# Moving sums from VectorE to GpSimd, two chunks' transposes from TensorE to VectorE and two chunks' keys through DRAM, with a new order of all steps

## The chip, the cores and the metric

The kernel runs on one NeuronCore of a Trainium2 chip. Its engines are TensorE (PE; PEld is its weight load), VectorE (DVE), ScalarE (ACT), GpSimd (POOL) and SyncE (SP), which here issues all the DMAs. The metric is the device time of one execution in microseconds (us), lower is better: before the change 535.64 us, the median of 3 runs (535.61 to 535.70).

## The reference

Two blocks follow each other. The first is a gated linear recurrence over 768 tokens, for 4 batches and 8 heads of 48 dimensions; the second is a feed-forward layer with the hardswish activation over the 3072 tokens that come out:

```python
for t in range(S):                                   # q, k, v, alpha: (4, 8, 768, 48)
    state = alpha[:, :, t, :, None] * state + einsum('bhd,bhe->bhde', k[:, :, t], v[:, :, t])
    y[:, :, t] = einsum('bhd,bhde->bhe', q[:, :, t], state)
x = y.transpose(0, 2, 1, 3).reshape(3072, 384)
h = x @ w_in                                         # (384, 2048)
g = h * clip(h + 3, 0, 6) / 6
out = g @ w_out                                      # (2048, 384)
```

## The kernel before

**Chunks.** The recurrence is done in 24 chunks of 128 tokens, six to a batch. For a chunk j the kernel needs alpha, k and q with the dimensions of a pair of heads on the partitions and tokens along the free axis. For chunks below FIRST (6) they arrive as tokens by dimensions and TensorE turns them (`transposed`, L274, four transposes of 128x128 for each of `ta`, `tk`, `tq`; ScalarE copies the turned alpha out, L300). From chunk FIRST on they arrive in a layout of 32x32 blocks (`load_akq`, four DMAs for each of alpha, k and q) and VectorE turns the blocks (`by_blocks`, L285, words `ca`, `tk`, `tq`). Two scans on VectorE give the running products of alpha (`r`, L309, and `p`, L320), and `scaled` (words `k` and `q`, L332) multiplies keys and queries by them.

**Attention of a chunk.** `sc` (L346) makes the scores on TensorE, `m` (L356) masks them on VectorE, `u` (L429) makes the update of the state, which `sm` (VectorE), `st` (L409, GpSimd) and `sv` (ScalarE) carry on, and `ya`, `yb` (L455) make the output, which `cy` copies to the feed-forward's input. `u` needs the keys by token. Below chunk FAR (8) TensorE turns the scaled keys back (`kb`, L374) and ScalarE copies them (`ck`). From FAR on VectorE turns 32x32 blocks (`kt`, L391), four DMAs write them to DRAM (`kw`, L396) and four read them back in the other layout (`kr`, L404).

**Feed-forward.** Tokens are taken in groups g of two chunks. The weights arrive as 64-bit numbers and are made into float32 by `d1`, `d2`, `dx` (ScalarE), `d3` (VectorE) and `d4` (L217, GpSimd). Group 0 and group 1 use plain products in the first layer (`fa`, `fb`, `f`), group 0 also in the second (`b`, L516). The other layers use schemes with fewer multiplications, in exchange for sums:

- First layer, groups 2 to 11: sums of weight blocks once (`y`, L577) and of input blocks for each group (`xc`, L586, 11 sums of 128x128), 20 products (`M`, L592 to L602, eight matmuls each), eleven products kept by ScalarE (`n`, L606), then 12 sums of 128x512 (`o`, L608; step 0 of outputs 2, 3, 6 and 7 adds two kept products, both in SBUF, and the last step adds a product that is still in PSUM). `e` (L494, ScalarE) and `h` (L498, VectorE) make the activation.
- Second layer, groups 1 to 11: sums of weight blocks once (`x`), sums of activations (`s`, L658: four of 128x512, one of 128x1024, one of two times 128x512), seven products (`P`, L685, sixteen matmuls each), copies `K` and sums `G` out of PSUM, stores `O`.

**Order.** The order is written out by hand as one long string of words (L751 to L900). A word is one call, such as `M.2.7.0` for product 7 of group 2 in PSUM bank 0. Each engine, and SP's DMA queue, takes its instructions in that order, and an instruction that waits holds back everything behind it on its engine. `z` is TensorE work without a use; 26 such products stand in the first 20 us, mostly ahead of and between the first chunks' transposes. PSUM has eight banks of 128x512: four are `banks` (attention), four are `bank_m` (feed-forward).

## Time and profile before

| | |
|---|---|
| median of 3 runs | 535.64 us |
| span of the profiled execution, first to last instruction | 533.7 us |
| the median over that span | 1.9 us |
| PE busy (6306 instructions) | 524.6 us |
| VectorE busy (849) | 477.2 us |
| ScalarE busy (503) | 257.2 us |
| GpSimd busy (71) | 50.4 us |
| granted TensorE clock | 1.00 throughout |
| DMA, 16 engines, mean share | 42.5% |

The span is a single profiled execution. Busy time of PE counts a matmul from its start to its modelled end, and matmuls overlap, so the rate of PE is read from the distance between the ends of equal instructions. VectorE's instructions overlap a little too: one of 0.68 us is followed by the next after 0.60 us.

### The profile page before, as it was taken

The page shows a single profiled execution, that of the slowest core. Times are in us where ns is not written, and L with a number is a line of the kernel's source. Part 1 is how long each engine was busy: PE and PEld are TensorE (multiplying, and loading weights), DVE is VectorE, ACT ScalarE, POOL GpSimd, SP SyncE. Part 2 cuts the span into 40 slices and gives each one's busy share as a digit, 9 for nine tenths or more (in the row PEclk, how much of TensorE's full clock was granted, in tenths as well). Part 3 has the DMA queues.
Part 4 walks back from the last instruction along what each step waited for, and adds up shares of the span by engine and source line. Part 5 has one row for each costly group of instructions (what it writes and reads, how often), then busy time and mean ns, then how long its engine had stood idle before and what let it go on. Part 6 is the DMA issues. An engine that isn't in the chain of part 4 may idle for free.

```text
span 533.7 us, 15143 instructions
## 1 busy us (share of the span) xinstructions
PE 524.6 (98%) x6306; PEld 499.4 (94%) x6306; DVE 477.2 (89%) x849; ACT 257.2 (48%) x503; POOL 50.4 (9%) x71
## 2 busy tenths in 40 slices
PE   8799999999999999999999999999999999999997
PEld 7698886789999999999999999999999999999997
DVE  6999989999999999998999999999999899496382
ACT  3889865212653553553544444642634544553340
POOL 5333425100000000000000000000000000000000
DMA  9998876005615155254344355044454042100001
GB/s 174 217 252 256 215 216 152 21 2 154 152 30 116 32 121 135 57 140 95 87 110 113 91 124 140 19 120 102 115 136 104 11 110 43 44 2 2 15 16 37
DMA packets 124100, 54.40 MB, mean 102 GB/s; under 512 B 83328, under 2 KB 116864, under 8 KB 124032
## 3 DMA queue, kind: packets, MB, share of 16 engines
q1 hardware_dynamic: 124032, 53.44, 42.5%
q8 instruction: 49, 0.80, 0.6%
q14 instruction: 19, 0.16, 0.1%
HBM read 44.50 MB, written 8.91 MB: 100 GB/s over the span
## 4 chain that ended last, share of the span: by engine, by line
PE 85%; DVE 8%; POOL 2%; DMA 2%; ACT 1%; issue 1%; SPq 1%; DVEq 0%; POOLq 0%
PE m_ps L703 34%; PE m_ps L600 34%; PE m_ps L478 5%; PE t_ps L455 4%; PE t_ps L346 2%; PE t_ps L429 2%; PE m_ps L489 2%; PE t_ps L282 1%; DVE rings L647 1%; DMA v<-in_v_dram 1%; DVE raw L537 1%; ACT raw L191 1%; DMA kq<-in_k_dram 1%; DVE g_sb L647 1%; DVE w L537 1%
## 5 line engine op out<-in xcount | busy, mean ns | idle before, releaser
L606 ACT COPY g_sb<-m_ps 128x512 f32<-128x512 f32 x110 | 63.6, 584 | 124.9 <-PE m_ps L600 104.1
L703 PE MATMUL m_ps<-w,g_sb 128*128 128x192 f32 x704 | 121.7, 327 | 0.0
L703 PEld LDWEIGHTS m_ps<-w,g_sb 128*128 128x128 f32 x704 | 113.7, 190 | 0.4
L703 PE MATMUL m_ps<-rings,g_sb 128*128 128x192 f32 x528 | 91.5, 326 | 0.0
L703 PEld LDWEIGHTS m_ps<-rings,g_sb 128*128 128x128 f32 x528 | 85.4, 190 | 0.1
L600 PE MATMUL m_ps<-xc,w 128*128 128x128 f32 x640 | 82.7, 277 | 0.3 <-DVE w L541 0.3
L600 PEld LDWEIGHTS m_ps<-xc,w 128*128 128x128 f32 x640 | 77.5, 192 | 1.5 <-issue 0.5
L494 ACT ACTIVATE r<-g_sb,half 128x512 f32<-128x512 f32 x80 | 56.8, 722 | 32.9 <-DVE g_sb L541 12.1
L498 DVE SCALAR_TENSOR_TENSOR g_sb<-r,g_sb 128x512 f32<-128x512 f32 x80 | 53.6, 682 | 4.6 <-ACT r L494 4.2
L600 PE MATMUL m_ps<-xT,raw 128*128 128x128 f32 x400 | 52.5, 277 | 0.0
L600 PEld LDWEIGHTS m_ps<-xT,raw 128*128 128x128 f32 x400 | 48.6, 192 | 0.6
L409 POOL TENSOR_TENSOR st<-sm,R 128x192 f32<-128x192 f32 x20 | 12.9, 643 | 353.8 <-DVE sm L439 306.7
L647 DVE TENSOR_TENSOR g_sb<-g_sb 128x512 f32<-128x512 f32 (+1 forms) x55 | 42.0, 795 | 0.2
L600 PE MATMUL m_ps<-xT,w 128*128 128x128 f32 x320 | 42.0, 276 | 0.0
L600 PEld LDWEIGHTS m_ps<-xT,w 128*128 128x128 f32 x320 | 39.3, 192 | 0.1
L366 ACT COPY A<-q 48x256 f32<-48x256 f32 x88 | 35.5, 404 | 5.0 <-DVE q L332 3.7
L356 DVE TENSOR_TENSOR A<-t_ps,mask 64x256 f32<-64x256 f32 x96 | 36.0, 414 | 0.4
L478 PE MATMUL m_ps<-xT,w 128*128 128x256 f32 x144 | 32.8, 382 | 0.0
L600 PE MATMUL m_ps<-xc,raw 128*128 128x128 f32 x240 | 31.8, 276 | 0.0
L309 DVE TENSOR_TENSOR_SCAN R<-t,ones 128x516 f32<-128x516 f32 x24 | 29.7, 1236 | 1.1 <-ACT t L300 1.0
L478 PEld LDWEIGHTS m_ps<-xT,w 128*128 128x128 f32 x144 | 26.7, 190 | 3.6
L600 PEld LDWEIGHTS m_ps<-xc,raw 128*128 128x128 f32 x240 | 29.6, 192 | 0.1
(104 smaller groups left out, 731.0 us busy)
## 6 DMA issues: line engine op xcount, KB each, us to landing
raw<-in_moe_w_out_dram SPq DMA_DIRECT2D x8, 768.0 KB, 5.2
raw<-in_moe_w_in_dram SPq DMA_DIRECT2D x6, 768.0 KB, 6.8
v<-in_v_dram SPq DMA_DIRECT2D x48, 96.0 KB, 3.0
out_dram<-oh SPq DMA_DIRECT2D x44, 96.0 KB, 1.7
far<-kq SPq DMA_DIRECT2D x64, 64.0 KB, 2.2
kb<-far SPq DMA_DIRECT2D x64, 64.0 KB, 2.0
aq<-in_alpha_dram SPq DMA_DIRECT2D x36, 96.0 KB, 2.5
qq<-in_q_dram SPq DMA_DIRECT2D x36, 96.0 KB, 2.4
```

The source lines that it names most:

```text
L309: nc.vector.tensor_tensor_scan(out=reverse(R, n - 1, n), data0=reverse(ax, n, n), data1=reverse(ones, n, n), initial=0.0, op0=ALU.mult, op ...
L356: nc.vector.tensor_tensor(out=to[:, a], in0=sc[a][half], in1=mask[half, half].unsqueeze(1).to_broadcast([HB, NP, HB]), op=ALU.mult)
L366: nc.scalar.copy(out=to[:, a], in_=Q_t[j][64 * a : 64 * a + D, :, half])
L409: nc.gpsimd.tensor_tensor(out=st, in0=sm, in1=R_t[j][:, :, 0:1].to_broadcast([C, NP, D]), op=ALU.mult)
L455: nc.tensor.matmul(y_of(j, (i + 1) // 2, p)[:, HB * b : HB * b + HB], vb[:, p, e : e + 32], A_t[j][:, b, 2 * p + a], start=(b == 0 and i = ...
L478: nc.tensor.matmul(h[:, f], w1[:, kk, o : o + C], xT_t[g][:, kk], start=(kk == 0), stop=(kk == KT - 1))
L494: nc.scalar.activation(out=to, in_=h, func=AF.Relu, bias=half, scale=1.0 / 6.0)
L498: nc.vector.scalar_tensor_tensor(out=to, in0=r, scalar=1.0, in1=h, op0=ALU.min, op1=ALU.mult)
L600: nc.tensor.matmul(acc[g][i][:, f * C : (f + 1) * C], spots[w][:, f * C : (f + 1) * C], x_of(g, x), start=(first and f == 0), stop=last, s ...
L606: nc.scalar.copy(out=slots[z], in_=acc[g][i])
L647: nc.vector.tensor_tensor(out=out, in0=in0, in1=in1, op=ALU.subtract)
L703: nc.tensor.matmul(to[g], a, rhs[:, f], start=(first and f == 0), stop=(last and f == HF - 1), skip_group_check=True)
```

## The change

- `FIRST` goes from 6 to 4: alpha, k and q of chunks 4 and 5 arrive in blocks and are turned by VectorE. Their six sets of four TensorE transposes and two ScalarE copies go; six VectorE block transposes come, and 24 DMAs of a quarter each in place of 6.
- `FAR` goes from 8 to 6: the keys of chunks 6 and 7 go through DRAM. Two sets of four TensorE transposes and two ScalarE copies go; two VectorE block transposes and 16 DMAs come.
- Words with a `g` in front (`gx`, `gy`, `gxc`, `go`, `gs`, `gk`, `gq`) run the same function with GpSimd in place of VectorE. The order uses 8 `gy`, 62 of the 110 `xc`, 30 of the 120 `o`, 38 of the 66 `s`, and 11 keys and 14 queries of `scaled`. That is 100 instructions of 128x512, 6 of 128x1024 and 62 of 128x128. All of them read two operands in SBUF.
- The eight PSUM banks are one set, `banks`, for attention and feed-forward.
- The order of the 1788 words is new from the first to the last. Apart from the `g` and the bank numbers the words are the same, but for `ta` of chunks 4 and 5 and `kb` and `ck` of chunks 6 and 7, which go, and `kt`, `kw` and `kr` of chunks 6 and 7, which come.

```diff
-    banks = [ps.tile([C, NP * C], FP, tag=f"t{i}", name=f"t{i}_ps") for i in range(4)]
+    banks = [ps.tile([C, NP * C], FP, tag=f"t{i}", name=f"t{i}_ps") for i in range(8)]
...
-    FIRST = 6
+    FIRST = 4
...
-        nc.vector.tensor_tensor(out=t, in0=src, in1=by, op=ALU.mult)
+        lane[0].tensor_tensor(out=t, in0=src, in1=by, op=ALU.mult)
...
-    FAR = 8
+    FAR = 6
...
-    bank_m = [ps.tile([C, GT * 2], FP, tag=f"m{i}", name=f"m{i}_ps") for i in range(4)]
...
-    def add(eng, out, in0, s0, in1, s1):
-
+    lane = [nc.vector]
+
+    def on_gpsimd(f):
+        def g(*at):
+            lane[0] = nc.gpsimd
+            f(*at)
+            lane[0] = nc.vector
+        return g
+
+    def add(out, in0, s0, in1, s1):
+        eng = lane[0]
...
-                nc.vector.tensor_tensor(out=t, in0=part(a21, i), in1=part(a22, i), op=ALU.add)
+                lane[0].tensor_tensor(out=t, in0=part(a21, i), in1=part(a22, i), op=ALU.add)
...
+    for name in ("x", "y", "xc", "o", "s", "k", "q"):
+        steps["g" + name] = on_gpsimd(steps[name])
...
-        run("""z.0.5 z.0.3 z.0.1 z.0.8 qa.0.0 w.0 d2.0 d3.0 la.0 ta.0.0 ca.0 r.0 lk.0 tk.0.1 k.0
-               z.0.2 p.0 la.1 ta.1.2 lq.0 tq.0.3 ca.1 r.1 lk.1 lv.0.0 sv.0.0 d1.0 kb.0.0 ck.0 z.0.2
...
+        run("""z.7.2 z.7.3 z.2.5 w.0 d2.0 d3.0 z.7.3 z.1.2 z.2.8 la.0 ta.0.7 ca.0 z.7.2 la.1 ta.1.0
+               ca.1 lq.0 tq.0.7 z.2.1 lk.0 tk.0.5 z.2.3 d1.0 dx.0 lk.1 w.2 r.0 p.0 q.0 qa.0.1 d1.2
...
+               sc.6.3.6 la.8 ca.8 K.1.2 gxc.2.1 gxc.2.3 gxc.2.10 gy.16 gy.17 gy.12 kr.6 u.6.5.7
...
+               m.8 gs.2.4 ca.11 M.3.9 o.3.1.0 n.3.5.10 P.2.5 tk.10 lq.11 e.3.1.1 h.3.1 sc.9.3.5
...
```

## The prediction

> **What bounds the kernel now.** I read the page first, its busy times and its 40 slices.
>
> ```profile
> span 533.7 us, 15143 instructions
> PE 524.6 (98%) x6306; PEld 499.4 (94%) x6306; DVE 477.2 (89%) x849; ACT 257.2 (48%) x503; POOL 50.4 (9%) x71
> ...
> PE   8799999999999999999999999999999999999997
> DVE  6999989999999999998999999999999899496382
> ```
>
> PE is busy all the time, and VectorE nearly so up to slice 32 (430 us). Next, who PE waited for (the view of waits, for PE alone):
>
> ```profile
> PE m_ps L532 <- POOL ident masks.py:199: 1.5, 1, 1.5
> PE t_ps L429 <- issue: 1.2, 2, 1.0
> PE t_ps L455 <- DVE s L439: 0.7, 1, 0.7
> PE m_ps L600 <- DVE w L541: 0.3, 1, 0.3
> ```
>
> The last is at 128 us, the others in the first 25. Whether a busy PE runs at its full rate is told by long runs of one instruction, in the chain of waits in order of time.
>
> ```profile
> 389.38 8.04 PE m_ps L600 x72
> 512.62 18.22 PE m_ps L703 x112
> ```
>
> 8.04/72 is 0.112 us for one matmul of 128 columns, 18.22/112 is 0.163 for one of 192. The same reading of ends gives 0.216 (256 columns) and 0.323 (384). Attention's small matmuls cost an entrance and an exit. The timeline of PE at 237 us shows it:
>
> ```profile
> 237.49 1.05 PE L600 MATMUL m_ps<-xc,w 128*128 128x128 f32 x8
> 238.47 0.69 PE L346 MATMUL t_ps<-q,k 48*64 48x64 f32 x32
> 238.99 0.63 PE L429 MATMUL t_ps<-v,kb 64*64 64x48 f32 x32
> 239.55 1.16 PE L600 MATMUL m_ps<-xT,raw 128*128 128x128 f32 x8
> ```
>
> The ends are 238.54, 239.16, 239.62 and 240.71: scores 0.62, update 0.46, and the product behind them 1.09 in place of 8 x 0.112 = 0.90. So leaving costs 0.19. Entering costs 0.15: scores that follow an update take 0.48. With these prices I added up PE's order. It gives 519.2 us to the last matmul, which ends at 530.8. The 11.6 us between them are waits: at 40 us PE is already 10.8 behind the sum, at 126 us still 10.8, later 0.4 at 128 us and next to nothing. The kernel is PE's work, plus a start of 10.8, plus 2.8 us of last copy and store.
>
> **The change part by part.** PE loses 24 transposes (alpha, k, q of chunks 4 and 5) and 8 (keys of 6 and 7).
>
> ```profile
> L282 PE MATMUL t_ps<-ident,rings 128*128 128x128 f32 x72 | 10.6, 279 | 1.1 <-DVE R L309 0.6 <-DVE sm L439 0.3 <-DVE A L356 0.2
> L374 PE MATMUL t_ps<-ident,k 128*128 128x128 f32 x32 | 4.9, 277 | 1.0 <-ACT t L300 0.7 <-ACT raw L186 0.3
> ```
>
> Their busy mean is 0.15, but four of them between products end 0.44 after the instruction in front, so 0.11 each: 32 x 0.11 = 3.5 us. The new order leaves attention for large matmuls 38 times where before it was 43: 1.0 for exits, 0.7 for entrances. PE's sum is 514.0, so **-5.2 us**. PE is the bound, so this is all on the path as long as nothing else makes it wait.
>
> VectorE gives up 100 sums of 128x512 (0.60 from end to end), 6 of 128x1024 (1.135) and 62 of 128x128 (0.20): 79.2 us. It takes six block transposes for chunks 4 and 5 (1.03) and two for the keys (0.62): 7.4. Its own work falls from 464 to 392, with waits for the port left out. ScalarE loses two copies of alpha and two of keys, at half load: nothing.
>
> GpSimd takes those 168. The rows nearest to them are its own:
>
> ```profile
> L409 POOL TENSOR_TENSOR st<-sm,R 128x192 f32<-128x192 f32 x20 | 12.9, 643 | 353.8 <-DVE sm L439 306.7 <-ACT v L419 47.1
> L217 POOL TENSOR_TENSOR w<-raw 128x768 int32<-128x768 int32 x11 | 17.7, 1608 | 32.4 <-DVE raw L210 15.2 <-ACT raw L186 6.7 <-issue 4.3
> ```
>
> Undisturbed, one is 0.515 and the other 1.465. A line through both has 0.195 us fixed and 1.65 ns a column: 1.04 for 512, 1.89 for 1024, 0.41 for 128. That is 104 + 11 + 25 = 141 us, so GpSimd is at 191 us, 36% of the span. Throughput is no bound. Ends: 0.89 for 512 (the float row alone, 0.515 plus 320 columns at an assumed 1.17 ns, VectorE's own slope) to 1.6 (the mean of L217 as it stands, for a third fewer columns).
>
> The cost is in VectorE's waits. The timeline, three spots (all engines):
>
> ```profile
> 92.51 1.69 POOL L217 TENSOR_TENSOR w<-raw 128x768 int32<-128x768 int32 x1 [3.76 <-DVE raw L210]
> 92.80 1.95 DVE L332 TENSOR_TENSOR q<-q,P 128x512 f32<-128x512 f32 x1
> ...
> 134.15 1.00 POOL L409 TENSOR_TENSOR st<-sm,R 128x192 f32<-128x192 f32 x1 [38.98 <-DVE sm L439]
> ...
> 278.90 1.20 DVE L309 TENSOR_TENSOR_SCAN R<-t,ones 128x516 f32<-128x516 f32 x1
> 278.95 1.47 POOL L409 TENSOR_TENSOR st<-sm,R 128x192 f32<-128x192 f32 x1 [24.93 <-DVE sm L439]
> ```
>
> A product of 0.68 took 1.95 behind GpSimd, and GpSimd's 0.515 took 1.47 behind a scan. It befell instructions that take two operands from SBUF (and L207); those that read PSUM (L498, L356 at 0.41) and block transposes kept their times beside GpSimd. While it runs, less its fixed 0.195, GpSimd keeps such instructions out: 0.85 for 512. Over the whole trace VectorE lost about 0.2 us for each us so kept (1.0 us after 120 us for 14 `st` of 0.32; 2.8 for 13 `d4` of 1.27).
>
> The Trainium skill, "SBUF — State Buffer", section "Who interferes with whom", speaks against this change: the pair of ports that VectorE and GpSimd share is an exclusive lock, and the loser blocks. The rows above agree (1.95 us for 0.68). Were every us that GpSimd holds the ports lost to VectorE, the stretch below would lose 32 us in place of 6.5. The same skill's "GPSIMD Engine Reference", section "Performance versus the Vector engine", has 4497 ns for a float32 sum of 2048 columns; at that slope, as an estimate, 512 take 1.3 and GpSimd's addition is 176 us in place of 141; no run here shows it.
>
> Where can lost VectorE time reach PE? I counted, for each wait of PE on VectorE, the VectorE work in front of it in the order, against PE's time at that step with a start of 10.8. The smallest margin shows what VectorE may idle, lose and hand over up to there. Before, it is 13.6 at 128 us, where PE did wait: 8.0 idle, 3.5 lost to `d4`, 2 of hand-overs. After: 12.4 at 124 us, 17.2 at 168, 19.5 at 185, 27 at 207, 45 at 285, 80 at 420. So danger lies between 95 and 190 us (words P.1.0 to M.4.0), where GpSimd gets 31 sums of 512, 1 of 1024 and 22 of 128 and keeps the ports for 32 us.
>
> The start moves. 23 `z` stand ahead of the first transpose where 17 did: 12 more matmuls of 0.112 put it at 9.3 us (before 7.94). From there I walked VectorE's order with the rows' durations (scan, reciprocal, scan, queries, keys, twice, then masks, `d3`): chunk 2's queries are ready at 27.7, before at 25.6, and PE, which has other work first, meets VectorE at 39 us some 0.8 to 1.2 later than before. I take **+1.0** (ends -0.5, if the early loads of alpha pay, and +2.5, the whole delay of the queries and the first weights).
>
> Lock: with that start the margins are 1.0 larger. At 124 us 13.4 stand against 7.2 idle in the start, 2.0 hand-overs, 3.0 for `d4` and 0.2 x 12.9 us held so far = 2.6: 1.4 short. At 168 18.2 against 12.4 + 4.8, at 185 20.5 against 12.7 + 6.5: enough. I take **+1.4**. Lower end 0 (GpSimd meets masks and transposes); at twice the share it is 4.0 at 124 and 5.2 at 185. A share below nothing is excluded, since the operation only adds.
>
> Loads: SP issues 506 DMAs in place of 472, at some 0.5 us each: 17 us of a queue that stands idle for 127 us on one kind of wait alone. Ahead of the weights w.5 to w.7 stand 0.33 MB more (two quartered loads read 352 KB for 192), 1.2 us at 268 GB/s; covered by the VectorE work that PE waits for there, 0 to 1.2. Keys of 6 and 7: write and read land 2.2 and 2.0 us after issue, `kr.6` is the word just ahead of `u.6`, and behind `la.8` on SP. The order gives 22 us of PE work from `kw.6` to `u.6`; 0, at most 4. Behind SP's waits nothing but loads two chunks ahead is queued. Hand-overs: turned keys go VectorE, GpSimd (`gk`), VectorE (`kt`), where VectorE stands for 1.04 that it did itself in 0.60: 5 times before 190 us, some 2 us of VectorE; 0 to 2 for PE. Banks in one set: the waits on them were under 0.3 us each; 0. The last stage: after the final product of group 11 one chain of sum, gate, product and sums runs to P.11.2, about 5.8 us; two products of 2.6 and the first half of the third cover it: 0 to 1.
>
> Sum: -5.2 + 1.0 + 1.4 = -2.8, a span of 530.9 in place of 533.7. The median lies 1.9 above its span: **532.8 us**.
>
> **The rivals.** *Port lock decides, slower.* Place: VectorE between 95 and 190 us. At 0.4 per us kept, 5.2 for PE, and with the start +1.0 it is 536.6; above that share it is slower than before, at 0.6 about 10 and 541. For it: VectorE is at 97% there before, and the share of its instructions with two SBUF operands is about half. Against: the share measured is 0.2, and the order gives VectorE work for 88% of the time from 124 to 185 us. *A wash.* The start costs its 2.5 and the lock 2.7, so that 535.6 results; for it, every margin is counted to about a us. *PE keeps its margin.* No wait but the start: 535.6 - 5.2 - 0.5 to + 1.0 = 529.9 to 531.4; for it, before, PE waited 0.4 us in 500. *The transposes were not on the path,* so that removing them brings nothing: 535.6 to 537; against it PE's sum, which follows the trace to 0.4 us from 40 us on. *The DRAM path holds `u.6`:* +4, 536.8.
>
> **How the numbers follow.** PE keeps most of its gain, 529.9 to 534.5: 0.60, and 532.8 is its middle. A wash within 0.2% (534.6 to 536.7, about what a measurement can tell from no change): 0.12. Slower: lock 0.20, DRAM, hand-overs and the start together 0.08. The range takes the first two and more than half of the third: 529.9 to 540. Faster 0.60, same 0.12, slower 0.28.
>
> **What would show it.** PE: 6274 matmuls, L282 x48, L374 x24, last matmul near 528. VectorE near 689 instructions, busy 410 to 430 with its losses; products and scans of over 1.3 us beside GpSimd. GpSimd near 190 to 230 busy, the 512s at 1.04 to 1.3. Waits of PE on VectorE or GpSimd near 124 us of 1 to 2 us. Wrong if PE's waits between 95 and 190 us add up to over 5, if `u.6` waits for its DMA, or if the first large products start later than 43 us.

## The result and the profile after

The changed kernel takes 552.25 us (median of 4 runs, 551.12 to 552.63). The kernel before, run beside it, takes 535.62. The ratio is 1.0309, with a 95% interval of 1.0294 to 1.0323: 3.1% slower, or 16.6 us. The forecast was 532.8, with a range of 529.9 to 540.0, so it was wrong in sign and in size. The profiled execution took 552.63 us with a span of 550.9.

The page of the kernel after, its busy times and three rows of its slices, against those shown of before:

```profile
span 550.9 us, 15151 instructions
PE 528.0 (96%) x6274; PEld 499.7 (91%) x6274; DVE 445.7 (81%) x689; ACT 257.3 (47%) x499; POOL 245.6 (45%) x239
...
PE   8689999999999999999979999999999999999997
DVE  6999999999999997989757898984986998552480
...
PEclk9999999999999999999979999999999999999999
```

PE has its 32 transposes less, and yet it is "busy" 3.4 us longer. VectorE's row has as many nines as before up to slice 15 (206 us) and gets room only behind that. The table of windows says it in numbers. First the kernel before, then after; the columns are the stretch, its length, and the busy time of PE, PEld, VectorE, ScalarE and GpSimd, then the clock and the DMAs.

```profile
0.00:100.00 100.00, 94.04 (x1142) 80.14 (x1143) 92.30 (x149) 70.71 (x115) 39.28 (x54) 1.00 0.87 200
100.00:200.00 100.00, 99.71 (x1229) 93.19 (x1231) 97.73 (x177) 42.20 (x89) 2.92 (x4) 1.00 0.35 81
200.00:300.00 100.00, 100.00 (x1221) 98.79 (x1214) 95.41 (x175) 45.12 (x94) 3.54 (x5) 1.00 0.45 106
```

```profile
0.00:100.00 100.00, 89.46 (x1012) 75.52 (x1013) 91.99 (x144) 66.14 (x102) 50.14 (x57) 1.00 0.86 204
100.00:200.00 100.00, 97.50 (x1327) 89.63 (x1326) 96.28 (x138) 44.54 (x96) 66.04 (x60) 1.00 0.47 111
200.00:300.00 100.00, 94.76 (x1107) 92.85 (x1107) 80.69 (x125) 40.62 (x85) 49.69 (x46) 0.97 0.45 106
```

In the first 200 us VectorE is as full as it was (188.3 us busy, before 190.0; e8 below shows how much of that is stretched instructions). GpSimd, which the prediction had at 36% of the span, is at 66% from 100 to 200 us. PE loses 4.6 us of busy time in the first 100, 2.2 in the second and 5.2 in the third.

The view of waits for PE shows which wait is the longest single one, and that it isn't where the prediction looked:

```profile
PE t_ps L429 <- DMA kb<-far: 3.8, 2, 3.6
PE t_ps L346 <- DVE q L332: 2.0, 1, 2.0
...
PE t_ps L477 <- DVE sm L439: 1.4, 1, 1.4
...
PE t_ps L346 <- POOL q L332: 0.8, 1, 0.8
```

L429 is the update `u`; it is `u.14`, at 279 us, that waits for its keys from DRAM. What follows is seen in windows of 2 us (PE's busy time first, the granted clock third from the end):

```profile
278.00:280.00 2.00, 0.98 (x36) 0.72 (x34) 1.34 (x1) 1.68 (x5) 1.91 (x3) 1.00 0.49 135
280.00:282.00 2.00, 0.00 (x0) 0.00 (x0) 0.00 (x0) 1.26 (x4) 0.00 (x0) 1.00 0.65 158
282.00:284.00 2.00, 1.27 (x32) 1.14 (x32) 0.00 (x0) 0.00 (x0) 0.00 (x0) 0.63 0.52 109
284.00:286.00 2.00, 2.00 (x18) 1.91 (x12) 1.72 (x4) 0.00 (x0) 0.35 (x1) 0.50 0.83 202
286.00:288.00 2.00, 2.00 (x9) 2.00 (x8) 1.36 (x4) 0.99 (x2) 0.16 (x1) 0.50 0.73 196
```

PE stands for 3.6 us, and then works for 6.8 us at a clock of 0.50: "busy", with half the matmuls. The stall costs twice.

To place the rest I used the prediction's own tool, the sum of PE's order, for each kernel: the start of each matmul in the trace less its place in the sum is how far PE is behind. The table has the lag in us at certain times of the trace, worked out in this way for the two kernels and for the experiments that follow. The sum itself is counted to the start of the last matmul. The lags hang on the prices of single matmuls and are good to 1 to 2 us.

| kernel | sum | 45 us | 95 | 135 | 207 | 250 | 290 | end |
|---|---|---|---|---|---|---|---|---|
| before | 518.8 | 10.7 | 10.8 | 11.3 | 11.8 | 11.9 | 11.9 | 11.8 |
| after | 513.6 | 13.4 | 15.2 | 17.7 | 20.6 | 22.6 | 29.9 | 33.7 |
| e14, more VectorE work in the start | 518.8 | 12.3 | 17.1 | 18.0 | 18.5 | 18.7 | 18.7 | 18.6 |
| e2, new layout, old order | 515.2 | 14.4 | 21.5 | 23.2 | 25.8 | 25.9 | 25.9 | 25.8 |
| e13, sums on GpSimd, old order | 518.8 | 10.7 | 10.7 | 14.9 | 16.7 | 16.8 | 17.5 | 19.4 |
| e8, after, no port | 513.6 | 14.3 | 15.7 | 20.1 | 22.4 | 25.4 | 30.8 | 33.9 |
| e9, after, no port, shorter | 513.6 | 14.2 | 16.7 | 17.0 | 17.4 | 19.0 | 24.9 | 26.4 |
| e12, as e9, reads early | 513.6 | 14.0 | 16.1 | 16.4 | 16.6 | 18.1 | 22.2 | 24.1 |

PE's sum fell by 5.2 us as forecast. Against that, PE falls behind by 4.4 us more than before up to 95 us, 4.4 up to 207, 1.9 up to 250, 7.3 up to 290 (the stall and its clock) and 3.9 in the rest: 22 us. With medians over all the profiles as prices the total is the same and the parts are 3.0, 6.1, 1.5, 8.3 and 3.1.

### The profile page after: what moved, and what is told of

Same layout as the page of the kernel before. It is cut to its first block, busy times and chain, and to the rows that moved or that the text cites. A ratio compares the mean times of both kernels' runs of the same rounds, so it can differ in the third digit from the quotient of the medians.

```text
span 550.9 us, 15151 instructions
## 1 busy us (share of the span) xinstructions
PE 528.0 (96%) x6274; PEld 499.7 (91%) x6274; DVE 445.7 (81%) x689; ACT 257.3 (47%) x499; POOL 245.6 (45%) x239
## 4 chain that ended last, share of the span: by engine, by line
PE 63%; DVE 17%; POOL 6%; issue 4%; SPq 4%; DMA 3%; ACT 2%; DVEq 0%; POOLq 0%; ACTq 0%
PE t_ps L711 28%; PE t_ps L608 27%; POOL g_sb L655 3%; PE t_ps L455 3%; DVE g_sb L497 2%; SPq L262 2%; PE t_ps L429 2%; PE t_ps L346 1%; PE t_ps L531 1%; DVE P L320 1%; SPq L404 1%; DMA kb<-far 1%; DVE rings L655 1%; DVE w L208 1%; DVE A L356 1%
## 5 line engine op out<-in xcount | busy, mean ns | idle before, releaser
L711 PE MATMUL t_ps<-w,g_sb 128*128 128x192 f32 x704 | 123.6, 330 | 1.2 <-POOL w L217 0.5
L711 PEld LDWEIGHTS t_ps<-w,g_sb 128*128 128x128 f32 x704 | 115.6, 193 | 2.9 <-DVE g_sb L497 0.9
L614 ACT COPY g_sb<-t_ps 128x512 f32<-128x512 f32 x110 | 64.0, 586 | 111.1 <-PE t_ps L608 85.5
L711 PE MATMUL t_ps<-rings,g_sb 128*128 128x192 f32 x528 | 92.1, 328 | 0.2 <-DVE oh L727 0.2
L711 PEld LDWEIGHTS t_ps<-rings,g_sb 128*128 128x128 f32 x528 | 85.2, 190 | 1.0 <-DVE oh L727 0.5
L608 PE MATMUL t_ps<-xc,w 128*128 128x128 f32 x640 | 84.0, 278 | 2.0 <-DVE xc L545 0.9
L493 ACT ACTIVATE r<-g_sb,half 128x512 f32<-128x512 f32 x80 | 56.8, 721 | 59.9 <-DVE g_sb L549 20.6
L608 PEld LDWEIGHTS t_ps<-xc,w 128*128 128x128 f32 x640 | 78.2, 191 | 3.9 <-DVE xc L545 0.8
L497 DVE SCALAR_TENSOR_TENSOR g_sb<-r,g_sb 128x512 f32<-128x512 f32 x80 | 63.6, 805 | 20.4 <-ACT r L493 18.7
L655 POOL TENSOR_TENSOR g_sb<-g_sb 128x512 f32<-128x512 f32 (+1 forms) x30 | 48.8, 1639 | 26.1 <-DVE g_sb L497 11.3
L608 PE MATMUL t_ps<-xT,raw 128*128 128x128 f32 x400 | 52.0, 276 | 0.0
L608 PEld LDWEIGHTS t_ps<-xT,raw 128*128 128x128 f32 x400 | 48.5, 192 | 0.1
L545 DVE TENSOR_TENSOR g_sb<-t_ps,g_sb 128x512 f32<-128x512 f32 x30 | 20.5, 683 | 14.9 <-ACT g_sb L614 13.5
```

The costliest lines, as they stand in the source:

```text
L493: nc.scalar.activation(out=to, in_=h, func=AF.Relu, bias=half, scale=1.0 / 6.0)
L497: nc.vector.scalar_tensor_tensor(out=to, in0=r, scalar=1.0, in1=h, op0=ALU.min, op1=ALU.mult)
L545: eng.tensor_tensor(out=out, in0=in0, in1=in1, op=ALU.add if s1 > 0 else ALU.subtract)
L608: nc.tensor.matmul(acc[g][i][:, f * C : (f + 1) * C], spots[w][:, f * C : (f + 1) * C], x_of(g, x), start=(first and f == 0), stop=last, s ...
L614: nc.scalar.copy(out=slots[z], in_=acc[g][i])
L655: lane[0].tensor_tensor(out=out, in0=in0, in1=in1, op=ALU.subtract)
```

## The experiments

The kernels are built from before or after; what is left out or added in each is said in its expectation. All ratios are to the kernel before, run on the same chip.

### Is it the sums, or the order? Each in the other's place

e1: after, with `lane[0]` left on VectorE. GpSimd was given 168 operations in all, 25 of them keys and queries; the expectations of e1 and e8 count these 25 twice.

```diff
         def g(*at):
-            lane[0] = nc.gpsimd
+            lane[0] = nc.vector
             f(*at)
```

> The kernel after, in its own order, with every sum and product that it gave to GpSimd done by VectorE again (168 sums and 25 scaled keys and queries). Nothing else changes. Theory A (GpSimd's sums and the port cost VectorE and PE their time): from 98 to 207 us, where PE fell 5.4 us behind its order's sum, at least 4 come back, and about half of the 3.8 lost behind 290 us, so 545 to 547 us; VectorE has 79 us more work of its own, and less than 5 us of stretched instructions in place of 35. Theory B (the new order costs the time, whichever engine does the sums): 551 or more, with the same waits of PE at u.14 (4.3 us) and at the start (2.9 us); if VectorE is now short, up to 560. The stall of u.14 and the slow matmuls behind it (7.3 us together) should stay under both, unless the order's timing moves the store of G.4.1.

Measured: 600.34 us, ratio 1.1196 (1.1162 to 1.1231). Neither theory held. The new order can't do without GpSimd; PE waits for VectorE all along:

```profile
PE t_ps L608 <- DVE xc L545: 13.4, 7, 4.0
PE t_ps L346 <- DVE q L332: 8.4, 2, 6.4
PE t_ps L374 <- DVE k L332: 6.9, 3, 5.4
```

So an order and the engines it was written for can't be judged apart by undoing one of them. The opposite test puts the same sums on GpSimd in the old order, which is independent of that.

e13: before, with `lane` in its code and a `g` before the words of the old order that have one in the new (160 of the 163).

```diff
-        add(nc.vector, x_of(g, 2 * KT + i), x_of(g, a), sa, x_of(g, b), sb)
+        add(lane[0], x_of(g, 2 * KT + i), x_of(g, a), sa, x_of(g, b), sb)
...
-    xc.2.1 x.3 y.4 y.8 xc.2.3
+    gxc.2.1 x.3 y.4 y.8 gxc.2.3
```

> The kernel before with its own order, layout and banks; only the sums that the change gives to GpSimd go there, at the places that they have in the old order (the same words, less the keys of chunks 4 and 5 and the queries of 4, which read PSUM here). Nothing is left out. The prediction's pricing: VectorE is relieved of 78 us and loses some 30 to the port, PE keeps its order, 535.6 to 538. Rival (hand-overs: GpSimd takes 1.27 us for 0.60 and 0.46 for 0.20, in chains that alternate between the two engines just ahead of a product; taking most of GpSimd's time away gave 7 us in the new order): 542 to 552, with PE waiting for sums of inputs and activations, for VectorE by name and for GpSimd.

Measured: 543.45 us, 1.0146 (1.0131 to 1.0161): 7.8 us slower. The rival is right in size. The largest wait is in the weight sums ahead of the first product:

```profile
PE m_ps L609 <- DVE raw L546: 2.3, 1, 2.3
...
PE m_ps L712 <- DVE g_sb L673: 1.3, 2, 0.8
```

e20: the same, with the 30 words ahead of `M.3.0` back on VectorE.

> As the run with the sums on GpSimd in the old order (543.5 us), but only the 130 words from the first product of group 3 on (about 170 us) go to GpSimd; the 30 ahead of it, the weight sums and the inputs of group 2, stay on VectorE. Nothing is left out. Theory (the sums cost where the margin is short, ahead of the first products of groups 2 and 3, and hardly where VectorE has room): most of the 7.8 goes, 536 to 538.5 us, PE on its sum as before until 170 us. Rival (the loss grows with the number of sums, by the port or by late hand-overs): 130 of 160 words keep 6 us, 541 to 543.

Measured: 539.32 us, 1.0064 (1.0048 to 1.0081). Half of the 7.8 was the early place (PE's stop of 2.3 us at 126 us and the slow clock behind it), the other half stays. It is spread thin: PE loses 0.4 to 0.9 at a time at 164, 274, 440 and 519 us, behind sums. Neither theory has it all. VectorE was relieved of 130 of the 160 words and is busy for 445.1 us in place of 477.2, which gave PE nothing, since PE had not waited for it there. How the rest divides between the port and late results is not shown by these two runs.

### The port

e3: before, with one sum on GpSimd behind each `n` of groups 3 to 11. e4: two memsets in its place.

```diff
     def keep1(g, i, z):
+        if g > 2:
+            nc.gpsimd.tensor_tensor(out=o_sb, in0=ones[:, 0:DM], in1=ones[:, C : C + DM], op=ALU.add)
```

> The kernel before, with 99 additional GpSimd sums of 128x384, which read two constants from SBUF and write a tile that nobody reads, one behind each kept product n of groups 3 to 11 (from about 200 us on). No result changes. It prices the port alone: by the fit of GpSimd's times they take about 1.0 us each, 100 us in all, of which about 80 us keep instructions with two SBUF operands out. The term of the prediction (VectorE loses 0.2 us for each us kept): VectorE's instructions are stretched by 16 us in all, and as VectorE was idle for 51 us, PE loses 0 to 3, so 536 to 539 us. Rival (a loser always blocks, share 0.6 and over): 48 us stretched, and PE loses 10 to 30 us, so 546 to 566.

> The kernel before, with two GpSimd memsets of 128x384 in place of each of the 99 dummy sums of the run beside it: GpSimd is as long at work, but reads nothing from SBUF. No result changes. If only instructions that read two SBUF operands hold the port against VectorE, VectorE keeps its times and the kernel stays at 535.6 within 0.5 us. If any GpSimd access holds it, VectorE stretches as in the run beside it.

The tile written, `o_sb`, turned out to hold a block of group 0's output that is stored late, so that block is overwritten in both. Measured: e3 556.77 us, 1.0394 (1.0373 to 1.0414), e4 536.0, 1.0001 (0.9992 to 1.0011). Groups of e3, busy us and mean ns behind the bar:

```profile
L606 POOL TENSOR_TENSOR o_sb<-ones 128x384 f32<-128x384 f32 x99 | 127.2, 1285 | 13.9 <-DMA out_dram<-o_sb 7.4
L498 DVE SCALAR_TENSOR_TENSOR g_sb<-r,g_sb 128x512 f32<-128x512 f32 x80 | 57.7, 734 | 3.0 <-ACT r L494 2.6
L309 DVE TENSOR_TENSOR_SCAN R<-t,ones 128x516 f32<-128x516 f32 x24 | 31.2, 1300 | 1.3 <-ACT t L300 1.2
```

and of e4:

```profile
L607 POOL MEMSET o_sb<- 128x384 f32 x198 | 82.7, 418 | 17.4 <-DMA out_dram<-o_sb 6.9
L498 DVE SCALAR_TENSOR_TENSOR g_sb<-r,g_sb 128x512 f32<-128x512 f32 x80 | 53.4, 680 | 4.4 <-ACT r L494 4.0
L309 DVE TENSOR_TENSOR_SCAN R<-t,ones 128x516 f32<-128x516 f32 x24 | 29.6, 1234 | 0.1
```

With memsets VectorE's rows are those of before (682 and 1236 ns); with sums they stretch. VectorE's busy time rises from 477.2 to 509.0 us, 32 us for 99 sums, 0.32 each. The rival's size is right (PE lost 21 us), though the share is not: a sum of 384 columns is 1.0 us undisturbed, by a line through GpSimd's 0.46 and 1.27 us for 128 and 512, and keeps VectorE out for 0.8 of it, so that the share is 0.4, twice the prediction's 0.2. In the old order VectorE was idle for only 16 us between 140 and 460 us to take it from. The Trainium skill, "SBUF — State Buffer", section "Who interferes with whom", says that a VectorE instruction with two SBUF inputs contends with a GpSimd instruction that reads SBUF and not with one that only writes it; these two runs agree.

What it costs in the kernel after is another question. e8: after, with each of GpSimd's sums replaced by the same operation on every 128th column and two memsets; e9: with one memset.

```diff
+    def pair(out, in0, in1, op):
+        if lane[0] is nc.vector:
+            nc.vector.tensor_tensor(out=out, in0=in0, in1=in1, op=op)
+            return
+        few = lambda x: x[:, :, 0:1] if len(x.shape) == 3 else x[:, 0 :: C]
+        nc.gpsimd.tensor_tensor(out=few(out), in0=few(in0), in1=few(in1), op=op)
+        for _ in range(2):
+            nc.gpsimd.memset(out, 0.0)
...
-        lane[0].tensor_tensor(out=out, in0=in0, in1=in1, op=ALU.subtract)
+        pair(out, in0, in1, ALU.subtract)
```

> The kernel after, in its own order, but each of the 193 sums and products that it gave to GpSimd is replaced there by the same operation on every 128th column and two memsets of the whole output: the same tiles are waited for and released, GpSimd is as long at work (about 1.25 us for 512 columns by the memset rows of the run with memsets), and it reads next to nothing from SBUF. The sums themselves are left out, so the outputs are not the reference's. Theory A (the port costs the time): the 30 us by which VectorE's instructions are stretched fall under 8, and PE gets back at least half of the 5.4 us lost between 98 and 207 us and of the 3.8 behind 290: 544 to 548 us, less if the chunk that feeds u.14 is also in time again (540). Theory B (GpSimd's own time, its queue and the order cost it, not the port): 550 to 553.

> As the run beside it, with one memset in place of two: GpSimd is done with each former sum in about 0.75 us in place of 1.25 (512 columns) and still reads next to nothing from SBUF. The sums are left out. What it gains on the run beside it is what GpSimd's slowness costs by late hand-overs alone. If hand-overs are as cheap as the prediction had them (0 to 2 us), it is 0 to 2 us faster than that run. If GpSimd's queue is what makes chunk 14's keys late (its 512s and one 1024 stood in front of the scaled keys from 245 to 255 us), u.14 no longer waits for its read from DRAM and the slow matmuls behind it go: 7 us faster. What then is left over 535.6 - 5.2 = 530.4 us belongs to the order and the start (4 us by the trace).

Measured: e8 550.58 us, 1.0287 (1.0269 to 1.0305); e9 544.97, 1.017 (1.0153 to 1.0187). The page of e8 shows how clean the first test is, and its first two stretches of 100 us go beside those of after (its clock of 0.95 is a slow stretch at 17 to 27 us):

```profile
PE 529.1 (96%) x6274; PEld 502.6 (91%) x6274; DVE 412.3 (75%) x689; ACT 257.2 (47%) x499; POOL 245.8 (45%) x575
...
0.00:100.00 100.00, 92.08 (x1011) 78.47 (x1012) 89.88 (x144) 65.98 (x102) 50.20 (x65) 0.95 0.87 203
100.00:200.00 100.00, 96.20 (x1313) 89.20 (x1312) 85.94 (x136) 42.42 (x92) 63.64 (x165) 0.98 0.48 111
```

GpSimd is as busy as in after (245.6), and VectorE is rid of 33 us of stretching. The median fell by 1.7 us, while the runs of each kernel are 1.5 to 2.3 apart (551.12 to 552.63, and 550.19 to 552.45). In the first 200 us VectorE is busy for 175.8 in place of 188.3, and PE gains nothing there: from 95 to 207 us it loses 6.7, in after 5.4. Theory A falls: the port stretches VectorE much as forecast, but in the new order VectorE has 92 us idle to pay with.

Halving GpSimd's operations brought another 5.6 us, most of it between 95 and 207 us (the lag at 207 us is 17.4 in place of 22.4). What went there is a stop of 2.4 us at 121 us, where `sc.6` waits for queries from GpSimd, and the slow clock behind it, 1.7. The kernel after, whose own stop there is 0.8, has no such slow clock. So the 7.3 us from after to e9 are what port and GpSimd's time cost together; how they share it is not settled. The stall of `u.14` did not go (3.5 us in e9), so it has another cause.

### The stall of u.14

SP's queue in the kernel after, 245 to 284 us (start, length of the issue, DMAs):

```profile
249.43 7.46 SPq L262 DMA_DIRECT2D aq<-in_alpha_dram  x8
260.18 3.78 SPq L396 DMA_DIRECT2D far<-kq  x4
...
268.11 2.57 SPq L396 DMA_DIRECT2D far<-kq  x4
270.73 3.34 SPq L262 DMA_DIRECT2D qq<-in_q_dram  x4
274.11 1.31 SPq L272 DMA_DIRECT2D v<-in_v_dram  x2
275.47 2.59 SPq L732 DMA_DIRECT2D out_dram<-oh  x3
278.16 1.30 SPq L272 DMA_DIRECT2D v<-in_v_dram  x2
279.51 2.00 SPq L404 DMA_DIRECT2D kb<-far  x4
```

From 260.2 us on SP issues without a pause, 0.5 to 0.9 us for each DMA. It had stood 3.5 us at `kw.14` (the first L396) until VectorE had turned the keys at 259.4, and before that, from 227 us on, 8.2 us at `kw.13` and 3.1 at the load of alpha. GpSimd had scaled chunk 14's keys behind three sums of activations of 1.8, 2.4 and 2.2 us, and was done with them at 255. The read `kr.14` (L404) is at the end of the backlog, and `u.14` starts at 282.6.

e5: after, with `kr.14` right behind `kw.15` (268 us). e6: also `lv.14`, `lq.16`, `lv.15` and `O.4.2` behind the copy `cy.12`, in this order.

```diff
-    kw.15 M.5.19 lq.16 ... lv.15.1 ... O.4.2 ... cy.12 ... O.4.1 M.5.14 O.4.0 ... lv.14.2 M.5.17 kr.14
+    kw.15 kr.14 M.5.19 ... cy.12 lv.14.2 lq.16 lv.15.1 O.4.2 ... O.4.1 M.5.14 O.4.0 ... M.5.17
```

> The kernel after, with one word moved: the read of chunk 14's keys from DRAM, kr.14, is issued right behind kw.15, ahead of the loads lv.14, lq.16, lv.15 and the stores O.4.2, O.4.1 and O.4.0, of which O.4.1 waits for VectorE's copy G.4.1. Theory: u.14 waited 4.3 us for this read because SP's queue stood at the store, and the gap let TensorE's clock drop, which cost 3.0 us more. Then both go: 545 us, and no slice with a clock under 9 tenths near 285 us. Rival: the wait only hides another one behind it (VectorE's work for u.14 and sc.14 is late in any case): 549 to 552, with PE waiting for VectorE at about 283 us.

> The kernel after, with five DMA words moved on SP's queue: the read of chunk 14's keys stands right behind the write of chunk 15's, and the loads lv.14, lq.16, lv.15 and the store O.4.2 follow once the output of chunk 12 is copied, so that both inputs of u.14 are issued ahead of what is needed later. The run before this one moved the keys alone, and u.14 then waited 4.4 us for lv.14. Theory (SP issued without a pause from 260 to 288 us, 28 us for work that a wait for kw.14 had held back, and u.14's inputs stood at its end): u.14 waits under 0.5 us, TensorE keeps its clock there, and 7.3 us come back: 545 us. Rival (PE has lost nothing that it would not lose at the next wait, since VectorE's chain behind u.14 is late too): 549 to 553.

Measured: e5 553.24 us, 1.0331 (1.0304 to 1.0357); e6 550.72, 1.0281 (1.0266 to 1.0297). In e5 `u.14` waits 4.4 us for `lv.14`, the other load in the backlog, and nothing is won. In e6 it waits for neither, and the next thing is late at 283 us, 2.2 us:

```profile
PE t_ps L711 <- ACT oh L724: 2.2, 1, 2.2
```

A product waits for its PSUM bank, which ScalarE's copy `G` has not cleared, and a slow clock follows again (1.7 us). Of the 7.3 us, 1.5 came back. e12, e9 with the words of e6:

> The kernel after with two edits that ran before, together: the short GpSimd operations that read almost nothing (545.0 us alone; the sums are left out) and the five moved DMA words that bring u.14's inputs earlier (550.7 alone, from 552.3). If the causes add, and the 3.5 us wait of u.14 and 2 to 3 us of low clock that the first still shows go too: 539 to 541. What then remains over the 530.4 us of PE's shorter order is the start, to 90 us, where the trace of the first has PE 8 us further behind than before. If u.14's wait hides VectorE's: 544 to 545.

Measured: 542.96 us, 1.0129 (1.0107 to 1.0151): 2.0 better than e9, with the same product waiting 2.1 us. The rival is nearer. Even with GpSimd's time and the port nearly taken away, the new order stays 7.3 us above the old kernel and 12.6 above what PE's shorter sum promised: by the table, 5.3 up to 95 us and 5.5 between 207 and 290. Of these 5.5, the product's wait and the slow clock behind it are 3.8; what the rest comes from stays open.

### The layout by itself

e2: before, with both layout changes. e11: FAR alone.

```diff
-    FIRST = 6
+    FIRST = 4
...
-    FAR = 8
+    FAR = 6
...
-    k.6 ... kb.6.0 ... ck.6 ... k.7 ... kb.7.3 ... ck.7
+    k.6 kt.6 kw.6 ... kr.6 ... k.7 kt.7 kw.7 ... kr.7
```

> The kernel before in its own order, with the two changes of layout alone: FIRST 4 (chunks 4 and 5 turned by VectorE, their transposes on PE gone) and FAR 6 (keys of chunks 6 and 7 through DRAM). No sums move to GpSimd. PE has 32 transposes of 0.11 us less, 3.5 us; VectorE has 7.4 us more, of which 7.3 stand before 140 us, where it was idle for 0.1 to 0.5 us in each 20. Theory (VectorE's margin of 0.4 us at 128 us is used up, and PE waits for the weights' sums): 538 to 541 us, PE waiting 5 to 7 us between 100 and 190 us. Rival (the prediction's pricing, each engine by itself): 532 to 533.

> The kernel before in its own order with FAR 6 alone: keys of chunks 6 and 7 through DRAM, 8 transposes of PE less (0.9 us), 1.24 us more for VectorE near 130 us, 16 more DMAs. By the prediction (DRAM path 0 to 4): 534.7 to 538. With the run that changes both layouts it tells which of the two costs the 11 us: if FIRST, this one is within 1.5 us of 535.6; if the DRAM path, it is above 540.

Measured: e2 546.81 us, 1.021 (1.0195 to 1.0225); e11 540.26, 1.009 (1.0073 to 1.0106). The removal of 32 transposes, 3.5 of the 5.2 us that PE's order gains, costs 11.2 us net in the old order, 4.6 by FAR and 6.6 by FIRST. For FAR the cause is plain. SP's queue in e11:

```profile
99.50 1.31 SPq L272 DMA_DIRECT2D v<-in_v_dram  x2
118.22 3.30 SPq L396 DMA_DIRECT2D far<-kq  x4
...
123.02 2.04 SPq L262 DMA_DIRECT2D aq<-in_alpha_dram  x4
```

and VectorE behind it:

```profile
127.07 1.08 DVE L286 STREAM_TRANSPOSE t<-aq 128x512 f32<-128x512 f32 x1 [1.77 <-DMA aq<-in_alpha_dram]
```

SP stands 17.4 us at `kw.7`; the alpha of chunk 8 behind it is issued at 123 us, before at 91; VectorE waits 1.8 us, PE 2.8, and the slow clock adds 1.7. e15 moves `kw.7` behind `la.8`:

```diff
-    kt.7 kw.7 ... lv.12.1 la.8 O.1.1
+    kt.7 ... lv.12.1 la.8 kw.7 O.1.1
```

> The kernel before with FAR 6 alone (540.3 us by itself), and one word moved: the write of chunk 7's keys, kw.7, stands behind the load of chunk 8's alpha, la.8, instead of ahead of it. In the run without the move, SP waited 17.4 us at kw.7 for VectorE's turned keys, la.8 was issued at 123 us in place of 91, VectorE stood 1.8 us for it, PE 2.8, and a slow clock behind that gap cost 1.7. Theory (a wait on SP's queue holds back a load that VectorE needs): VectorE does not wait for alpha, PE waits under 1.2 us near 128 us, no slow clock: 535.0 to 536.3. Rival (the 1.3 us of added block transposes alone use up VectorE's margin and PE waits the same): 539 to 540.5.

Measured: 536.88 us, 1.0023 (1.0014 to 1.0032). The time is 0.6 us above the theory's range, and the mechanism held: one word on SP's queue was 3.4 of the 4.6. PE's wait near 128 us is 1.05, and no slow clock follows. What is left, 1.3 us over before, still eats the 0.9 that PE gained.

e19, the keys of chunks 6 and 7 scaled by GpSimd on top of that (`k.6`, `k.7` become `gk.6`, `gk.7`):

> The run with keys of chunks 6 and 7 through DRAM and alpha ahead of the write (536.9 us), with the two products of the keys of chunks 6 and 7 on GpSimd, which is idle there: VectorE has 1.2 us less ahead of 128 us, where PE waited 1.05. Nothing is left out. Theory (VectorE's margin decides): PE's wait under 0.4 us, 535.0 to 536.0, level with the kernel before or 0.1% faster. Rival (GpSimd's 1.2 us for 0.60 makes the turned keys late, or the port takes it back): 536.9 or more.

Measured: 537.34 us, 1.0028 (1.0018 to 1.0039), PE's wait 1.02. The theory fell. VectorE is spared 1.2 us there, and PE waits as long. No version here beats the kernel before.

For FIRST there are two candidates, VectorE's six turns and the loads in blocks. e14 adds VectorE time without the loads, e17 takes most of the turns' time away and keeps the loads:

```diff
+    def dummy():
+        for _ in range(2):
+            nc.vector.tensor_tensor(out=o_sb, in0=ones[:, 0:DM], in1=ones[:, C : C + DM], op=ALU.add)
```

> The kernel before with 12 additional VectorE sums of 128x384 of constants, two behind each word ca, tk and tq of chunks 4 and 5, where the run with the new layout alone has its block transposes: about 5.6 us of VectorE in place of 6.2, with PE's transposes and the loads as before. Nothing is left out. Theory (up to 100 us VectorE has no room, and what is added there reaches PE whole or more, also by the weights and chunks behind it): 541 to 547, PE falling behind between 30 and 95 us. Rival (the quartered loads made that run slow, not VectorE): 535.6 to 538.

> The kernel before in its own order with both layout changes (546.8 us by themselves), with the six block transposes of chunks 4 and 5 cut to a quarter (part of the turning is left out) and kw.7 behind la.8. What is left of the layout change is its loads, its DMA issues and PE's 3.5 us gain. Theory (VectorE's 6.2 us and the held-back load made the 11 us): 533 to 536.5. Rival (the quartered loads, which read 1 MB more in the first 90 us, make the weights late): 539 to 543, with PE waiting for weights from GpSimd near 50 us.

Measured: e14 542.4 us, 1.0125 (1.011 to 1.014); e17 541.09, 1.01 (1.0077 to 1.0122). Both candidates are real. The 12 sums were longer than expected, 7.9 us of VectorE from end to end (0.59 each, and three stretched), and cost PE 6.8, nearly all of it by 135 us: in the old order VectorE's time up to there reaches PE at 0.86 for one. With the turns cut, e17 is still 4.2 us above e15, and PE has 2.6 us less to do than there, so the loads, with the quarter of the turns that stays, cost 6.8. They don't act where the rival said; it is ScalarE that gets its weights late (waits of ScalarE, 22 to 60 us, e17; in before there is none on a DMA, and none in e2 either, where the whole turns make other things late first):

```profile
ACT w L196 <- DMA raw<-in_moe_w_in_dram: 3.4, 2, 2.0
ACT w L196 <- DMA g_sb<-in_moe_w_in_dram: 1.0, 1, 1.0
```

The two overlap: FIRST in whole made PE wait for 6.6 + 2.6 = 9.2 us; 6.8 and the 5.3 of VectorE's 6.2 us at 0.86 would be 12.1.

e16, the same cut of the turns in the new order:

```diff
-        nc.vector.transpose(out=to.rearrange("r p (u v) -> r p v u", v=V),
-                            in_=quads[name, j % NQ][:, :, :, 0:BLK])
+        n = 1 if 4 <= j < 6 else V
+        nc.vector.transpose(out=to.rearrange("r p (u v) -> r p v u", v=V)[:, :, 0:n],
+                            in_=quads[name, j % NQ][:, :, 0:n, 0:BLK])
```

> The kernel after in its own order, with the six block transposes of alpha, keys and queries of chunks 4 and 5 cut to the first quarter of their columns, so that VectorE has about 4.5 us less between 30 and 100 us; loads and waits stay. Part of the turning is left out, so the outputs are not the reference's. Theory (VectorE's time in the start is on the path also in the new order): PE, 4.4 us further behind at 95 us than before, regains 3 to 5 there, and the time is 547 to 549.5. Rival (the start's loss is the order's own, or loads; or u.14's late read swallows what is gained): 551 to 553.

Measured: 553.04 us, 1.0317 (1.0301 to 1.0333). The theory fell here: in the new order the start does not get better with less VectorE time. Whether its 4.4 us are the loads or the order of its words stays open.

### What a gap of PE costs

e18: before, with five stops of PE.

```diff
+    def gap(m, n):
+        nc.tensor.matmul(banks_m(m), o_sb[:, 0:C], ident, start=True, stop=True)
+        for _ in range(n):
+            nc.gpsimd.memset(o_sb, 0.0)
+        nc.tensor.matmul(banks_m(m), o_sb[:, 0:C], ident, start=True, stop=True)
...
+    banks_m = lambda m: bank_m[m][:, 0:C]
```

> The kernel before with five stops of PE of growing length, one ahead of the first product of each of groups 4 to 8: two small matmuls, and between them 2, 3, 4, 6 and 8 GpSimd memsets of a tile that both read (0.42 us each), so that PE stands for about 1.0, 1.5, 1.9, 2.7 and 3.5 us. A stored tile of group 0 is overwritten; no time depends on it. It prices a gap of PE by itself: in the runs so far a gap of under 1.8 us left the clock at 1.00, of 2.0 to 2.9 mostly cost 1.7 us at a clock of 0.50, of 3.0 to 6.4 us 1.5 to 3.4. Theory: the first two or three stops leave the clock alone, the last two are each followed by 3.4 to 6.8 us at 0.50; sum of the stops 10.6 and of the slow stretches 3.4 to 5 us, 549 to 552. Rival (the slow clock came with VectorE's or the DMAs' state, not with PE's gap): no slow stretch, 546.

Measured: 551.97 us in one run. The stops were 1.02, 1.55, 2.02, 2.92 and 3.87 us. The third was followed by 3.4 us at half clock; the two longer ones were not. So neither theory had it: a stop alone does bring the slow clock, but its length doesn't decide. The windows show what may. Each is 3.41 us long, and they are laid so that an edge falls on the change of clock at 279.23 us:

```profile
275.82:279.23 3.41, 1.39 (x12) 1.20 (x12) 3.41 (x7) 1.95 (x4) 1.68 (x4) 1.00 0.39 114
279.23:282.64 3.41, 3.41 (x17) 3.41 (x17) 3.41 (x7) 0.53 (x2) 0.00 (x0) 0.50 0.63 142
...
320.19:323.61 3.42, 1.45 (x13) 1.26 (x11) 3.42 (x6) 1.17 (x2) 1.67 (x4) 1.00 0.58 139
323.61:327.02 3.41, 2.46 (x18) 2.46 (x19) 3.38 (x8) 0.81 (x2) 1.64 (x3) 1.00 0.03 12
364.57:367.98 3.41, 1.44 (x10) 1.25 (x8) 3.38 (x7) 0.00 (x0) 1.68 (x5) 1.00 0.59 171
367.98:371.40 3.42, 1.52 (x12) 1.52 (x13) 0.00 (x1) 0.06 (x1) 1.67 (x4) 1.00 0.61 156
```

The third stop lies in one window, in which PE is idle for 2.02 us. An edge cuts the fourth and the fifth, so that no window holds more than 1.97. The last section has the count over all the traces.

## Why the prediction was wrong, point by point

**PE's order sum, -5.2: held.** 518.8 to 513.6; L282 has 48 and L374 24 transposes. Whether a shorter sum alone shortens the kernel is not shown: every version that has it (e2, e11, e15, e17) waits for more than it gains.

**"As long as nothing else makes it wait": the clause in which everything lay.** In the old order VectorE is idle for 8.6 us of the first 180, and e14 shows that a microsecond more there costs PE 0.86. The prediction credited VectorE with 79 us given up in whole; the windows show VectorE as full as before up to 200 us, of which 12.5 us are stretched instructions (188.3 less e8's 175.8). The relief came where PE had not been waiting: e13 and e20 relieve VectorE of most of it and are slower. The margins that I counted (12.4 at 124 us, 45 at 285, 80 at 420) let VectorE run ahead of PE as far as the order has work, as if no load, product or GpSimd result had to come first. After 200 us VectorE is idle for tens of us in short waits for GpSimd, ScalarE and PE. So the step that failed most is the one from VectorE's relief to PE's path, by margins counted as VectorE's work against PE's time: the sum had PE fall behind by 2.4 us, and it fell behind by 22.

**Start, +1.0 (ends -0.5, +2.5): 2.7 at 45 us, 4.4 at 95.** At 45 us about its upper end, at 95 above it. The longest wait is 2.0 us at 20 us for the queries `q.1`; VectorE makes them behind the mask of chunk 0, as in the old order, where PE has an update to do in between and does not wait for them. VectorE's turns are not the cause of the rest (e16), which stays open.

**GpSimd's price, 1.04 us for 512.** It is 1.27 undisturbed (1.18 for the products of keys and queries), 2.36 for 1024, 0.46 for 128; inside the range, above the value taken. The line through an integer row of another shape was the weaker guide; the estimate from the Trainium skill, "GPSIMD Engine Reference", section "Performance versus the Vector engine", was 1.3. GpSimd is busy 245.6 us, not 191.

**"Throughput is no bound", hand-overs 0 to 2: wrong.** 36% was a mean over the span; from 100 to 200 us it is 66%, and shortening the operations alone gave 5.6 us (e8 to e9), of which 4.1 are one stop and its slow clock. In the old order nearly the same sums cost 7.8, the port's share included.

**The port, +1.4: at most some 1.7 in all (e8), and nothing where it was put.** The stretching was near what the prediction took, 33 us for some 135 us kept (0.25 each, forecast 0.2). That it reaches PE between 95 and 190 us is not what e8 shows, so the near agreement of 1.4 and 1.7 is luck. As the deciding rival the port falls. That it was no danger in general was luck of the idle time too: in the old order 99 sums of 384 columns cost 21 us (e3).

**Loads, 0 to 1.2: most of 6.8 in the old order (e17),** where ScalarE's weights come late. I had hidden them behind VectorE's work, which was itself late.

**DRAM path, 0 to 4 at `u.6`: nothing at `u.6`, 3.6 at `u.14`.** The step that failed is "behind SP's waits nothing but loads two chunks ahead is queued". I took SP's idle time for room. Waits at two writes and one load stop the queue for 14.8 us between 227 and 260 us, and then SP issues for 28 us without a pause. e11 and e15 show the same with one word, worth 3.4 us.

**Banks, 0: hidden, not free.** Behind the stall of `u.14` a product waits 2.2 us for a bank (e6).

**No term at all: the clock.** 3.4 us behind the one stall, and 1.7 in most of the experiments that had one.

**The forecast's form.** The terms' upper ends add up to about +11 over the kernel before, the range to 540 took in 4.4 of that, and no end held the stall with its clock. The chance of 0.28 for slower rested on one mechanism, the port, which was not it.

By parts, measured alone in the old order: layout +11.2 (PE's -3.5 in it), sums +7.8, together 19.0; in the new order, 16.6. If the two add, which no run shows, the new order recovers some 2.4 us of what they cost. It can't be run without the sums on GpSimd (e1).

## What to carry to other kernels

Relief for a full engine counts only in the stretch in which another waits for it: make the table of busy time by stage, before and after, and price each edit in its own stage, never by the sum or the mean over the span. When an edit puts a waiting DMA write on a queue, list the loads queued behind it and who needs them. And price every stall of PE above some 2 us with the slow clock that may follow it.

## What the runs showed of the hardware that I had not expected

**A stop of PE halves its clock when about 2 us of it fall into one window of 3.41 us.** In every trace the stretches between two changes of clock are whole multiples of 3.41 us (3.41, 6.83, 10.24, up to 112.64 and more). I divided the 19 traces that have such a change into windows of 3.41 us from it. In 18 windows at full clock PE was idle for 1.99 us or more, by the modelled ends of its matmuls, and each was followed by 0.50. Of some 2900 others 10 were, four with 1.60 to 1.97 us idle and six in the first 23 us with 1.45 to 1.47, where others with as much kept the clock. So the length of a stop tells less than where it falls. Of 27 stops of 2.00 to 6.43 us, 21 were followed by a stretch at 0.50, which cost 1.5 to 1.7 us in 15 cases and 2.2 to 3.4 in six; 2.00, 2.15, 2.23, 2.27, 2.92 and 3.87 us went free, and an edge cuts each of them. Of 45 stops from 1.02 to 1.99 us, one (1.99) was followed by it, and five stand in a slow stretch of the start that had begun before them. The Trainium skill, "TensorE: Matmul & The Clock Gate", "Part 1: The HAM clock gate", has half the clock after an idle window of about 3.4 us that runs on its own. Half the clock and the windows of 3.41 us agree; a window need not be idle as a whole, since 2 us in it were enough here.

**A write that waits on SP's queue costs far from where it stands.** 17.4 us of waiting at one write moved a load by 32 us and cost 1.8 us on VectorE, 2.8 on PE and 1.7 of clock, two engines and one chunk away.

**The same stretching of VectorE by the port costs 21 us or at most some 1.7.** 32 us of it in a kernel whose VectorE is idle for 16 us from 140 to 460 us (e3), 33 us in one that has 92 idle in all (after against e8).
